# Fused attention and two MLPs: softmax transposes moved to the ends of slots, a pair's value products gathered in one slot, the norm's transposes in every other slot, the opening slots reordered

## The chip, the cores and the metric

One core of one Trainium2 chip runs the whole program. The metric is the device time of one execution in microseconds (us), the median of several runs. TensorE is written PE, VectorE DVE, ScalarE ACT, GpSimd POOL, and SyncE, which issues most of the DMAs, SP.

## The reference

The inputs are q, k and v of shape (4, 8, 576, 64), and the weights of two MLPs. All arrays are fp32.

```
scores = q @ k^T / sqrt(64)                        # per batch and head
scores = where(0 <= i - j < 128, scores - slope_h * |i - j|, -1e9)
a = exp(scores - max(scores)); a = a / (sum(a) + 1e-9)
x = (a @ v), heads side by side                    # (2304, 512)
h = x @ w_in                                       # (2304, 2048)
y = (h * clip(h + 3, 0, 6) / 6) @ w_out            # (2304, 512)
xn = y / sqrt(mean(y*y) + 1e-6) * rms_g
out = (silu(xn @ w_gate) * (xn @ w_val)) @ w_out2  # inner width 1536
```

A query sees only the 128 keys up to itself, so a tile of 128 queries needs two tiles of keys.

## The kernel before, in words

The 2304 tokens are 18 tiles of 128, in six **blocks** of three tiles. The order of all instructions is written out by hand, and each engine runs its own queue in that order; waits come from the data and from the tiles' buffers alone.

**Products.** The MLPs' matmuls run in fp32r, each fp32 operand split into a high and a low part, with three products for one. A **slot** of the first MLP is one 128-wide piece `m` of the inner width for one block: `product1` (12 matmuls of 384 columns into `ps_h`, one buffer), the activation into `g` (ACT Relu L599, DVE L600, ACT cast L605, DVE subtraction L611), and `product2` (nine matmuls of 512 columns into three `ps_o` tiles) of the slot before, which `finish1` issues. `PARTS` gives the order: block 0 up to piece 12, block 1, the rest of block 0, then blocks 2 to 5. Slots are counted by `t`; the first 15 (`AHEAD`) hold attention alone, the other 96 hold products too. The second MLP follows with no attention in it.

**Attention** runs in the slots ahead of the block that needs it. Two heads are a **pair**; a pair of a block has three **steps**, one for each tile of queries, u = 0, 1, 2. A step goes through S (scores on PE, `bias` on DVE, `exp` on ACT, the reciprocal `r` on POOL), D (`divide`, DVE), T (up to four transposes on PE into `ps_t`, and `weights`, the copy to `pt` on ACT) and V (`values`, up to eight matmuls into the pair's `ps_av`). After the last V, `finish` casts the pair's result on ACT and DVE. Q is the scaling (L247) or splitting (L253 to L260) of the pair's q and k. The table `plan` says in which slot, counted from the pair's first slot `t0`, each step does each part. Pairs of blocks 0 and 1 take three slots and overlap; those of blocks 2 to 5 (16 pairs) take four. Inside a slot of the first MLP, PE's order is `product1`, T, S, V, `product2`, then the norm's transposes.

**Norm.** When a block's first MLP is done, `Norm` evicts the three `ps_o` tiles, squares each (ACT L446), takes the factor on POOL, scales (DVE L454), transposes (four transposes into `ps_x`, issued by `back` at a slot's end) and copies (`store`, ACT L460, at the next slot's start; then a DMA to DRAM), one tile a slot. `ps_t` and `ps_x` are the same single PSUM buffer "T", so a transpose into it waits for the ACT copy of what stood there.

**Weights.** First-MLP weights come as 16 units of raw words, converted by ACT and DVE (`W1.step`, L116 to L132) through the slots of block 0. Second-MLP weights are converted through blocks 2 to 4 (`W2.finish`, the same lines, ACT's L130 writing a single buffer `wt`) and stored to DRAM by SP; when the last block of the first MLP starts, POOL fetches the first two converted tiles back (`W2.fetch`, L209) into space that attention has used.

**Opening.** Before the first slot, `busy(WARM)` issues five matmuls on a constant (each runs as two), and each of the 15 opening slots has one more, so that PE isn't idle. In an opening slot DVE's order is bias, the end of `finish`, the q scaling, divide.

Of the kernel before, what the change touches and what calls it, by code (L numbers as in the profile page):

```python
# [21 lines left out]
B, H, S, D = 4, 8, 576, 64  # L22
# [5 lines left out]
M1, M2 = F1 // P, F2 // P  # L28
# [7 lines left out]

CUT = 12

WARM = 5
PARTS = [(0, 0, CUT), (1, 0, M1), (0, CUT, M1)] + [(b, 0, M1) for b in range(2, len(BLOCKS))]  # L40

STARTS = {b * S // P for b in range(B) if b * S % P == 0}
# [4 lines left out]
PARTS_OF = ((0, 0), (0, 1), (1, 0))  # L47

AHEAD = 3 * H // 2 + 3

OPEN = {"reuse_waits": "tile"}


def f32(ap):
    return ap.bitcast(F32)
# [3 lines left out]
def fused_kernel(ctx: ExitStack, tc: tile.TileContext, qd, kd, v, w1, w2, rms_g, out):  # L59
# [10 lines left out]
    wpool = ctx.enter_context(tc.tile_pool(name="wpool", bufs=M1))  # L70
# [144 lines left out]
    W1, W2 = First(), Second()  # L215
# [143 lines left out]

    pairs = [Pair(b, j) for b in range(len(BLOCKS)) for j in range(H // 2)]
    slots = {kind: {} for kind in "QSDTV"}
    for k, pr in enumerate(pairs):
        b, j = divmod(k, H // 2)
        if b < 2:
            t0, plan = 3 * j if b == 0 else AHEAD - 3 + 3 * j, {"S": (0, 1, 2), "D": (1, 2, 3), "T": (2, 3, 4), "V": (3, 4, 5)}
        else:
            t0, plan = AHEAD + M1 * (b - 1) - 4 + 4 * j, {"S": (0, 0, 2), "D": (1, 1, 3), "T": (2, 3, 4), "V": (4, 4, 6)}
        slots["Q"].setdefault(t0 - 1, []).append(pr)  # L370
        for u in range(pr.n):
            step = Step(pr, u)
            for kind, at in plan.items():
                slots[kind].setdefault(t0 + at[u], []).append(step)

    def at(t):
        return [slots[kind].get(t, []) for kind in "QSDTV"]

    def prepare(pairs_, steps):

        for pr in pairs_:
            pr.split() if pr.parts else pr.scale()
        for x in steps:
            k = pairs.index(x.pair) + 2
            if x.last and k < len(pairs):
                pairs[k].load()
# [26 lines left out]
    def product2(outs, g, w, m, last, first=0):  # L413

        for i, o in enumerate(outs):
            for a, b in ((0, 0), (0, 1), (1, 0)):
                pe.matmul(  # L417
                    o,
                    lhsT=g[:, a, i * P : (i + 1) * P],
                    rhs=w[:, b],  # L420
                    start=(m == first and a == 0 and b == 0),
                    stop=(m == last and a == 1),
                )

    class Norm:
# [28 lines left out]
                vec.tensor_scalar(self.y[t], self.y[t], self.ri[t], None, ALU.mult)  # L454

        def store(self):
            k = self.t - 2
            if k in self.ps:
                yt = ypool.tile([P, KC, P], F32, tag="yt", name="yt", bufs=2)
                act.copy(yt, self.ps.pop(k))  # L460
                i = BLOCKS[self.b][0] + k
                d = dram.tile([P, KC, P], F32, tag=f"x2_{i}", name=f"x2_{i}")
                sp.dma_start(out=d, in_=yt)
                x2[i] = d
# [26 lines left out]
    def busy(n):  # L491
        for _ in range(n):
            pe.matmul(warm[:, : 2 * P], lhsT=rel[:, :P], rhs=rel, start=True, stop=True)  # L493

    busy(WARM)
    pairs[0].scale()
    for t in range(AHEAD):
        q, s_, d_, t_, v_ = at(t)
        scores(s_, t % 2)
        for x in t_:  # L500
            x.transpose()
        for x in v_:
            x.values()
        busy(1)
        for x in t_:
            x.weights()
        for x in s_:
            x.bias()
        for x in v_:
            if x.last:  # L510
                x.pair.finish()
        prepare(q, s_)
        for x in d_:
            x.divide()
        for x in s_:
            x.exp()
        if t == 2:
            W1.load(3)
        W1.step(0, *{4: (0,), 5: (1, 2), 7: (3,), 9: (4, 5)}.get(t, ()))
        W1.step(1, *{8: (0,), 11: (1, 2)}.get(t, ()))  # L520


    pend = None
    norms, partial = [], []

    def finish1():

        nonlocal outs
        b, m, m0, m1, g = pend
        if m == m0:  # L530
            outs = [ps_out.tile([P, DM], F32, tag="o", name="ps_o") for _ in range(BLOCKS[b][1])]
        product2(outs, g, W1.w_out(m), m, m1 - 1, m0)
        norms[:] = [x for x in norms if x.back()]
        if m == M1 - 1:
            norms.append(Norm(b, outs, partial if m0 else None))
        elif m == m1 - 1:
            for i, o in enumerate(outs):
                y = x0pool.tile([P, DM], F32, tag=f"part{i}", name="part")
                if i % 2:
                    act.activation(y, o, AF.Copy, scale=1.0 / 6.0)  # L540
                else:
                    vec.tensor_scalar(y, o, 1.0 / 6.0, None, ALU.mult)
                partial.append(y)

    def load_x2(b):
        i0, n = BLOCKS2[b]
        raw = p2x.tile([P, KC, 3 * P], F32, tag="x2raw", name="x2raw")
        for i in range(n):
            sp.dma_start(out=raw[:, :, i * P : (i + 1) * P], in_=x2[i0 + i])
        return raw  # L550
# [8 lines left out]
        )  # L559
        return t  # L560

    outs, slot = None, AHEAD
    for p, (b, m0, m1) in enumerate(PARTS):
        n = BLOCKS[b][1]
        last = p == len(PARTS) - 1
        nq = n * P
        if p == 2:
            conv.close()
            ypool = ys.enter_context(tc.tile_pool(name="ypool", bufs=3, **OPEN))
        if last:  # L570
            second.close()
            ys.close()
            att.close()
            ypool = p2.enter_context(tc.tile_pool(name="ypool2", bufs=3, **OPEN))
            wpool2 = p2.enter_context(tc.tile_pool(name="wpool2", bufs=2, **OPEN))
            p2x = p2.enter_context(tc.tile_pool(name="p2x", bufs=1, **OPEN))
            W2.fetch(2, wpool2)
        xs = xs_of[b]
        for m in range(m0, m1):
            t, slot = slot, slot + 1  # L580
            q, s_, d_, t_, v_ = at(t)
            if p == 3 and m == 2:
                first.close()
                wcpool = second.enter_context(tc.tile_pool(name="wcpool", bufs=1, side="right", **OPEN))
                W2.load()
                W2.load()
            for x in norms:
                x.store()
            ps = ps_h.tile([P, 4 * P], F32, tag="h", name="ps_h")
            product1(ps, W1.w_in(m), xs, n)  # L590
            for x in t_:
                x.transpose()
            if s_:
                scores(s_)
            for x in v_:
                x.values()
            g = gpool.tile([P, 2, 3 * P], F32R, tag="g", name="g")
            r = gpool.tile([P, 3 * P], F32, tag="t", name="t", bufs=1)
            act.activation(r[:, :nq], ps[:, :nq], AF.Relu, bias=three)  # L599
            vec.scalar_tensor_tensor(out=r[:, :nq], in0=r[:, :nq], scalar=6.0, in1=ps[:, :nq], op0=ALU.min, op1=ALU.mult)  # L600
            for x in t_:
                x.weights()
            for x in d_:
                x.divide()
            act.copy(g[:, 0, :nq], r[:, :nq])  # L605
            for x in s_:
                x.bias()
            for x in v_:
                if x.last:
                    x.pair.finish()  # L610
            vec.tensor_sub(g[:, 1, :nq], r[:, :nq], f32(g[:, 0, :nq]))  # L611
            for x in s_:
                x.exp()
            for x in norms:
                x.scale()
            prepare(q, s_)
            if p < 2:
                k = m + 1 if p == 0 else CUT + 1 + m
                W1.load(k + 3)
                if k < M1:  # L620
                    W1.step(k + 1, 0)
                    W1.step(k, 3, 4)
                    W1.step(k + 1, 1, 2)
                    W1.step(k, 5)
            if p == 3 and m == 3:
                W2.begin()
            if not last and (p == 3 and m > 3 or p > 3 and m % 4 != 0):
                W2.finish()
            if last:
                if m == M1 - 4:  # L630
                    raw = load_x2(0)
                if m == M1 - 1:
                    xs2 = [split_x2(0, raw, c) for c in range(KC)]
            if pend:
                finish1()
                if last and m:
                    W2.fetch(1, wpool)
            pend = b, m, m0, m1, g


# [13 lines left out]
    for b, (_, n) in enumerate(BLOCKS2):  # L654
        nq = n * P
        xs, xs2 = xs2, []
        for m in range(M2):
# [24 lines left out]
            pend = b, m, g  # L682
# [43 lines left out]
```

## Time and profile before

| | us |
|---|---|
| median of 3 runs | 1025.15 (1024.11 to 1025.45) |
| the profiled execution's own time | 1025.17 |
| its span, first to last instruction | 1023.4 |

The profile is of one execution. "Busy" is the time in which an engine has an instruction in flight; a timeline row gives the start, the time, the engine and its line, output and inputs, the count of merged instructions, and in brackets the idle time before it with what ended it. PE's matmuls overlap at their ends, so the length of a group is read from its start to the next group's start. "PEclk" is the granted share of TensorE's 2.4 GHz.

### The profile page before, as it was taken

What the parts mean: (1) busy time and instruction counts of PE and PEld (TensorE: products, weight loads), DVE (VectorE), ACT (ScalarE), POOL (GpSimd) and SP (SyncE); (2) the same over time, 40 slices, a digit from 0 to 9 for tenths busy, and PEclk for the clock granted to TensorE, in tenths of its full rate; (3) what the DMA queues carried; (4) which work ended last, traced back from release to release, by engine and by line L of the source; (5) the groups of instructions that cost most, each with busy time, mean ns of one, the idle gap of its engine ahead of it and who ended that gap; (6) DMA issues with size and microseconds to landing.
All of it is one profiled execution on the core that took longest, in us unless ns stands there. A gap on an engine that the chain in (4) does not pass through costs nothing.

```text
span 1023.4 us, 14712 instructions
## 1 busy us (share of the span) xinstructions
PE 1001.1 (98%) x5668; PEld 885.4 (87%) x5668; DVE 458.5 (45%) x1096; ACT 433.0 (42%) x952; POOL 115.5 (11%) x219
## 2 busy tenths in 40 slices
PE   8999899999999999999999999999999999999998
PEld 5577688888888788788899899999999999999997
DVE  5588764355787677766422312222222222222212
ACT  5699854356667665764432422112111122111111
POOL 4233111122212211220211100000000000000000
PEclk9899999999999999999999999999999999999999
DMA  6445401113675565543597300100100100200000
GB/s 216 136 183 195 191 29 32 55 39 125 210 234 179 186 210 175 189 160 124 200 334 247 124 21 1 62 1 1 62 1 1 62 1 1 62 2 1 31 1 31
DMA packets 49238, 105.28 MB, mean 103 GB/s; under 512 B 3856, under 2 KB 28432, under 8 KB 44816
## 3 DMA queue, kind: packets, MB, share of 16 engines
q1 hardware_dynamic: 46576, 85.47, 24.8%
q0 software_dynamic: 2592, 18.88, 5.5%
q8 instruction: 44, 0.72, 0.3%
q14 instruction: 26, 0.21, 0.1%
HBM read 76.02 MB, written 28.31 MB: 102 GB/s over the span
## 4 chain that ended last, share of the span: by engine, by line
PE 87%; DVE 6%; ACT 5%; issue 2%; DMA 1%; POOL 0%; ACTq 0%; POOLq 0%; DVEq 0%
PE ps_o L417 31%; PE ps_h L404 16%; PE ps_g L404 15%; PE ps_v L404 15%; PE ps_av L349 3%; PE ps_t L336 3%; PE ps_s L296 2%; PE ps_s L287 1%; DVE wx L128 1%; ACT w L130 1%; PE warm L493 1%; DVE t L600 1%; ACT wx L121 1%; DVE w L132 1%; ACT t L599 1%
## 5 line engine op out<-in xcount | busy, mean ns | idle before, releaser
L417 PE MATMUL ps_o<-w,g 128*128 128x512 f32 x1512 | 385.0, 398 | 5.6 <-DVE w L132 2.8
L417 PEld LDWEIGHTS ps_o<-w,g 128*128 128x128 f32 x1512 | 277.5, 188 | 67.6 <-DVE w L132 5.4
L404 PE MATMUL ps_h<-xs,w 128*128 128x384 f32 x1152 | 219.6, 338 | 1.8 <-DVE t L600 1.7
L404 PEld LDWEIGHTS ps_h<-xs,w 128*128 128x128 f32 x1152 | 203.5, 188 | 9.6 <-DVE t L600 2.6
L667 DVE TENSOR_TENSOR t<-t,ps_v 128x384 f32<-128x384 f32 x72 | 39.9, 554 | 306.0 <-PE ps_v L404 306.0
L404 PE MATMUL ps_g<-xs,w 128*128 128x384 f32 x864 | 163.8, 337 | 0.4 <-ACT xs L555 0.2
L404 PE MATMUL ps_v<-xs,w 128*128 128x384 f32 x864 | 161.5, 334 | 0.0
L404 PEld LDWEIGHTS ps_g<-xs,w 128*128 128x128 f32 x864 | 153.1, 188 | 7.4 <-ACT xs L555 0.7
L404 PEld LDWEIGHTS ps_v<-xs,w 128*128 128x128 f32 x864 | 151.0, 188 | 0.0
L600 DVE SCALAR_TENSOR_TENSOR t<-t,ps_h 128x384 f32<-128x384 f32 x96 | 53.2, 554 | 148.1 <-ACT t L599 148.1
L664 ACT ACTIVATE t<-ps_g 128x384 f32<-128x384 f32 x72 | 35.4, 492 | 192.5 <-PE ps_g L404 192.3
L669 ACT CAST g<-t 128x384 fp32r<-128x384 f32 x72 | 36.9, 513 | 162.3 <-DVE t L667 162.3
L599 ACT ACTIVATE t<-ps_h,three 128x384 f32<-128x384 f32 x96 | 55.2, 575 | 102.7 <-PE ps_h L404 102.5
L322 ACT ACTIVATE t<-t,m 128x256 f32<-128x256 f32 (+1 forms) x144 | 69.2, 483 | 11.9 <-DVE m L310 11.9
L324 POOL TENSOR_SCALAR r<-den 128x2 f32<-128x2 f32 x72 | 28.9, 402 | 341.3 <-ACT t L322 339.9
L130 ACT CAST w<-wx 128x512 fp32r<-128x512 f32 (+1 forms) x52 | 39.1, 751 | 57.8 <-DVE wx L128 42.5
L605 ACT CAST g<-t 128x384 fp32r<-128x384 f32 x96 | 49.3, 514 | 33.0 <-DVE t L600 26.9
L325 POOL TENSOR_TENSOR r<-r,minus 128x2 f32<-128x2 f32 x72 | 59.3, 823 | 6.0
L611 DVE TENSOR_TENSOR g<-t,g 128x384 fp32r<-128x384 f32 x96 | 53.2, 554 | 13.1 <-ACT g L605 12.0
L670 DVE TENSOR_TENSOR g<-t,g 128x384 fp32r<-128x384 f32 x72 | 40.2, 558 | 41.7 <-ACT g L669 41.7
L132 DVE TENSOR_TENSOR w<-wx,w 128x512 fp32r<-128x512 f32 (+1 forms) x52 | 44.1, 848 | 13.4 <-ACT w L130 13.4
L310 DVE CUSTOM_DVE_ANT_0 t<-ps_s,rel 128x256 f32<-128x256 f32 (+2 forms) x128 | 44.8, 395 | 10.7 <-PE ps_s L296 9.0
(63 smaller groups left out, 711.5 us busy)
## 6 DMA issues: line engine op xcount, KB each, us to landing
wraw<-w SPq DMA_DIRECT2D x36, 512.0 KB, 4.6
w<-w SPq DMA_DIRECT2D x36, 512.0 KB, 3.2
w<-w POOLq DMA_DIRECT2D x18, 1024.0 KB, 5.3
wraw<-w SPq DMA_DIRECT2D x16, 1024.0 KB, 8.7
kraw<-kd SPq DMA_DIRECT2D x20, 256.0 KB, 2.7
vraw<-v SPq DMA_DIRECT2D x20, 256.0 KB, 4.1
qraw<-qd SPq DMA_DIRECT2D x24, 192.0 KB, 2.8
x<-yt SPq DMA_DIRECT2D x18, 256.0 KB, 2.2
```

Of the source, the lines that this page charges most:

```text
L130: act.copy(t[:, 0], x)
L132: vec.tensor_sub(t[:, 1], x, f32(t[:, 0]))
L310: vec.tensor_tensor_reduce(out=self.t[:, a, c0:], in0=s[:, c0:], in1=(rel_split if self.i in SPLITS else rel)[:, c0:], scale=2.0 ** (-8.0 ...
L322: act.activation(p, p, AF.Exp, bias=self.m[:, a : a + 1], scale=-1.0, accum_out=self.den[:, a : a + 1])
L325: pool.tensor_tensor(self.r, self.r, minus, ALU.pow)
L404: pe.matmul(ps[:, : n * P], lhsT=w[:, a, c * P : (c + 1) * P], rhs=xs[c][:, b, : n * P], start=(k == 0), stop=(k == 3 * KC - 1),)
L417: pe.matmul(o, lhsT=g[:, a, i * P : (i + 1) * P], rhs=w[:, b], start=(m == first and a == 0 and b == 0), stop=(m == last and a == 1),)
L599: act.activation(r[:, :nq], ps[:, :nq], AF.Relu, bias=three)
L600: vec.scalar_tensor_tensor(out=r[:, :nq], in0=r[:, :nq], scalar=6.0, in1=ps[:, :nq], op0=ALU.min, op1=ALU.mult)
L605: act.copy(g[:, 0, :nq], r[:, :nq])
L611: vec.tensor_sub(g[:, 1, :nq], r[:, :nq], f32(g[:, 0, :nq]))
L670: vec.tensor_sub(g[:, 1, :nq], r[:, :nq], f32(g[:, 0, :nq]))
```

## The change

The plan of blocks 2 to 5 becomes: T of u = 1 in slot `t0 + 3` as before, behind `product1` and with no scores in that slot; T of u = 0 and u = 2 under a new kind L, issued behind `product2` (and the norm's transposes) at the very end of slots `t0 + 1` and `t0 + 3`, their `weights` copies on ACT at the next slot's start (`late`); V of all three steps in slot `t0 + 4`, which is the next pair's `t0`. `finish` of a pair so falls in the same slot. The norm's `scale` and `back` run only in slots an even number past the 15th (`go`) from block 2 on, in every slot before that and in the last block; `store` copies whatever was transposed. `finish1` moves ahead of `W1.step` and `W2.finish` in program order. In the opening and block 0, Q moves one slot earlier for the pairs of blocks 0 and 1; q scaling and divide go ahead of `finish`; `WARM` is 3.

```diff
-WARM = 5
+WARM = 3
...
-            t0, plan = AHEAD + M1 * (b - 1) - 4 + 4 * j, {"S": (0, 0, 2), "D": (1, 1, 3), "T": (2, 3, 4), "V": (4, 4, 6)}
-        slots["Q"].setdefault(t0 - 1, []).append(pr)
+            t0, plan = AHEAD + M1 * (b - 1) - 4 + 4 * j, {"S": (0, 0, 2), "D": (1, 1, 3), "T": (None, 3, None), "L": (1, None, 3), "V": (4, 4, 4)}
+        slots["Q"].setdefault(t0 - (2 if b < 2 else 1), []).append(pr)
...
         def store(self):
-            k = self.t - 2
-            if k in self.ps:
+            for k in list(self.ps):
...
+        prepare(q, s_)
+        for x in d_:
+            x.divide()
         for x in v_:
             if x.last:
                 x.pair.finish()
-        prepare(q, s_)
-        for x in d_:
-            x.divide()
...
-        norms[:] = [x for x in norms if x.back()]
+        if go:
+            norms[:] = [x for x in norms if x.back()]
...
+            go = p < 3 or last or (t - AHEAD) % 2 == 0
...
+            for x in late:
+                x.weights()
+            late = l_
             ps = ps_h.tile([P, 4 * P], F32, tag="h", name="ps_h")
             product1(ps, W1.w_in(m), xs, n)
...
-            for x in norms:
-                x.scale()
+            if go:
+                for x in norms:
+                    x.scale()
             prepare(q, s_)
+            if pend:
+                finish1(go)
+                if last and m:
+                    W2.fetch(1, wpool)
+            for x in l_:
+                x.transpose()
...
-            if pend:
-                finish1()
-                if last and m:
-                    W2.fetch(1, wpool)
```

## Rows read from the trace of the kernel before

**Rows 1.** The page, busy time of the engines over the span.
```profile
PE 1001.1 (98%) x5668; PEld 885.4 (87%) x5668; DVE 458.5 (45%) x1096; ACT 433.0 (42%) x952; POOL 115.5 (11%) x219
```
**Rows 2.** Waits of PE: total us, times, longest us.
```profile
PE ps_t L336 <- ACT yt L460: 4.9, 4, 1.5
PE ps_s L296 <- DVE qraw L247: 2.9, 4, 0.9
...
PE ps_o L417 <- ACT part L540: 2.6, 1, 2.6
...
PE ps_h L404 <- DVE t L600: 1.7, 1, 1.7
```
**Rows 3.** Timeline of PE: slots of one pair, and a slot with values alone.
```profile
362.36 2.27 PE L404 MATMUL ps_h<-xs,w 128*128 128x384 f32 x12
364.46 0.60 PE L336 MATMUL ps_t<-ident,t 128*128 128x128 f32 x4
364.99 0.98 PE L287 MATMUL ps_s<-ks,qs 64*128 64x256 f32 x12
365.90 1.09 PE L349 MATMUL ps_av<-pt,vraw 128*64 128x128 f32 x16
366.92 2.34 PE L417 MATMUL ps_o<-w,g 128*128 128x512 f32 x9
369.10 2.27 PE L404 MATMUL ps_h<-xs,w 128*128 128x384 f32 x12
...
373.29 2.27 PE L404 MATMUL ps_h<-xs,w 128*128 128x384 f32 x12
...
379.20 2.27 PE L404 MATMUL ps_h<-xs,w 128*128 128x384 f32 x12
...
383.83 2.27 PE L404 MATMUL ps_h<-xs,w 128*128 128x384 f32 x12
...
484.17 2.27 PE L404 MATMUL ps_h<-xs,w 128*128 128x384 f32 x12
486.37 0.66 PE L349 MATMUL ps_av<-pt,vraw 128*64 128x128 f32 x8
486.95 2.33 PE L417 MATMUL ps_o<-w,g 128*128 128x512 f32 x9
```
**Rows 4.** Timeline of DVE: divides in the slot that starts at 369.10.
```profile
372.49 1.14 DVE L330 TENSOR_SCALAR t<-t,r 128x256 f32<-128x256 f32 x4
```
**Rows 5.** Timeline of PE and ACT around the norm of block 2.
```profile
336.28 0.66 PE L336 MATMUL ps_t<-ident,t 128*128 128x128 f32 x4 [1.53 <-ACT yt L460]
...
335.04 0.62 ACT L446 ACTIVATE junk<-y 128x512 f32<-128x512 f32 x1
...
335.65 0.57 ACT L460 COPY yt<-ps_x 128x512 f32<-128x512 f32 x1
```
**Rows 6.** Timeline of PE in the opening slots.
```profile
2.17 4.63 PE L493 MATMUL warm<-rel 128*128 128x256 f32 x10 [2.17 <-POOL rel L93]
...
19.39 0.49 PE L296 MATMUL ps_s<-kraw,qraw 64*128 64x128 f32 x4 [0.87 <-DVE qraw L247]
```
**Rows 7.** Stretches: us, busy by engine, PEclk, DMA share, GB/s.
```profile
33.00:35.20 2.20, 1.40 (x12) 0.71 (x10) 1.36 (x7) 2.00 (x9) 0.92 (x2) 1.00 0.69 210
35.20:42.30 7.10, 7.04 (x30) 3.94 (x30) 3.82 (x16) 3.39 (x9) 2.39 (x4) 0.52 0.12 37
```
**Rows 8.** Timeline of PE and DVE in slots 28 to 30, behind block 0's first part.
```profile
131.17 2.27 PE L404 MATMUL ps_h<-xs,w 128*128 128x384 f32 x12
...
130.26 1.14 DVE L330 TENSOR_SCALAR t<-t,r 128x256 f32<-128x256 f32 x4
...
141.31 0.61 DVE L330 TENSOR_SCALAR t<-t,r 128x256 f32<-128x256 f32 x2
```
**Rows 9.** Timeline of ACT and POOL at the last block's start.
```profile
497.46 0.62 ACT L130 CAST w<-wx 128x512 fp32r<-128x512 f32 x1 [4.25 <-DMA w<-w]
...
487.36 1.32 POOL L209 DMA_DIRECT2D w<-w  x2 [16.53 <-PE ps_av L349]
```

More of the change, by code (lines that the diff above doesn't have):

```diff
@@ L49 @@
 AHEAD = 3 * H // 2 + 3
+KINDS = "QSDTLV"
 OPEN = {"reuse_waits": "tile"}
@@ L362, in fused_kernel @@
     pairs = [Pair(b, j) for b in range(len(BLOCKS)) for j in range(H // 2)]
-    slots = {kind: {} for kind in "QSDTV"}
+    slots = {kind: {} for kind in KINDS}
     for k, pr in enumerate(pairs):
@@ L373, in fused_kernel @@
             for kind, at in plan.items():
-                slots[kind].setdefault(t0 + at[u], []).append(step)
+                if at[u] is not None:
+                    slots[kind].setdefault(t0 + at[u], []).append(step)
     def at(t):
-        return [slots[kind].get(t, []) for kind in "QSDTV"]
+        return [slots[kind].get(t, []) for kind in KINDS]
     def prepare(pairs_, steps):
@@ L497, in fused_kernel @@
     for t in range(AHEAD):
-        q, s_, d_, t_, v_ = at(t)
+        q, s_, d_, t_, _, v_ = at(t)
         scores(s_, t % 2)
@@ L524, in fused_kernel, with finish1 @@
     norms, partial = [], []
-    def finish1():
+    def finish1(go=True):
         nonlocal outs
@@ L560, in split_x2 @@
         return t
-    outs, slot = None, AHEAD
+    outs, slot, late = None, AHEAD, []
     for p, (b, m0, m1) in enumerate(PARTS):
@@ L580, in fused_kernel @@
             t, slot = slot, slot + 1
-            q, s_, d_, t_, v_ = at(t)
+            q, s_, d_, t_, l_, v_ = at(t)
+            go = p < 3 or last or (t - AHEAD) % 2 == 0
             if p == 3 and m == 2:
```

## The prediction

> **What bounds the kernel now.** I read the page first: PE is busy for 98% of the span [rows 1], so only what PE does, or waits for, can move the end. The second view is the waits of PE. They are few and have four main causes: a softmax transpose that waits for the norm's copy out of the shared PSUM buffer (4.9 us), scores that wait for the scaled q (2.9 us), a product that waits for the eviction of block 0's partial result (2.6 us) and one that waits for an activation (1.7 us) [rows 2]. The third is PE's timeline, which gives each group's price as the distance from its start to the next group's start [rows 3]. The reader is to see how regular this is: a slot without attention takes 4.19 us (369.10 to 373.29), whatever other engines do. The fourth is the granted clock by stretches: it is 1.00, 2.4 GHz, but for one stretch of 7.1 us in the opening at 0.52, mostly the 1.2 GHz level, right behind a stretch in which PE was busy for 1.40 of 2.20 us [rows 7]. So the change is worth what it takes out of PE's row: waits, the price of groups, and the slow stretch.
>
> **Values in one slot.** Sixteen matmuls of V take 1.02 us (365.90 to 366.92), eight take 0.58 (486.37 to 486.95) [rows 3]: 0.44 for each further eight, 0.14 once. A pair had 16 in one slot and 8 in another, 1.60 us; 24 together are 1.46 by that line. 16 pairs x 0.14 = 2.3 us. If instead each step costs 0.58 wherever it stands, 24 cost 1.74, and 2.3 us are lost; if the fixed part is twice what I read, 4.5 are gained. I take 2.3, on the line through the two rows.
>
> **Transposes moved.** T ahead of scores costs 0.53 us (364.46 to 364.99). T with nothing else in its slot makes that slot 4.63 instead of 4.19 (379.20 to 383.83): 0.44. Scores or values that stand directly behind product 1 begin 2.20 after its start (484.17 to 486.37), transposes 2.10 (362.36 to 364.46): 0.10 more [rows 3]. So taking T from ahead of S saves 0.53 and costs 0.44 + 0.10: nothing. The trace has no scores that follow product 1 in these slots, so I keep 0.1 either way for 2 T in 16 pairs, +-3 us.
> What a T at a slot's end can lose is a wait: all behind it in PE's queue, the next slot's product 1 first, stands still. T of u = 0 now ends slot t0 + 1, whose divides come late: in the slot that starts at 369.10 they start at 372.49 and take 1.14 us for four [rows 4]. The two of u = 0 are done at about 373.06; T's place is behind product 2, at 373.29 [rows 3]. The cover is 0.23 us, so I cost it at nothing. T of u = 2 has only its own two divides ahead of it and a T of u = 1 in its slot: more cover. The copies of these T run on ACT at the next slot's start, ahead of its Relu, while PE is in product 1 for 2.1 us; V, their first reader, stands behind the scores.
>
> **The norm.** T of u = 1 waited up to 1.53 us for the copy of the norm's tile, since ACT had a square (335.04) and a weight piece ahead of the copy (335.65, 0.57 us) [rows 5]. Every other slot leaves only the second tile of a block with a T in the middle of the next slot. There ACT now has the square ahead of the weight piece, filling what was idle time, and `finish` is gone from that slot on DVE and ACT; I estimate that 0.15 remains, in three blocks (none to 1.5 each). One new wait comes: in slot 46 `go` still holds in each slot, a norm's transpose and a T follow each other directly, and the second must wait for the copy between them, 0.57 plus about 0.2 for the hand-over. Sum: 4.9 - 0.45 - 0.75 = 3.7 us (0 to 4.9).
>
> **The opening.** Four matmuls of the warm-up go: ten took 4.63 us [rows 6], so 1.85 us if PE stays at that slow pace, half of it (0.9) if the clock rises at the same moment as before. The first softmax chain on DVE, ACT and POOL then becomes the limit for a moment; I take 1.2 (0.5 to 1.9). q is scaled a slot earlier, and scaling and divide no longer stand behind `finish`, so the waits as at 19.39 go [rows 2, 6]: 2.9 at most. ACT is close to full in these slots, and the divide that follows the scaling is the next in line, so I take 2.2 (0 to 2.9). The slow stretch came right behind the last of these waits. With PE denser it should not come: 7.1 us x 0.48 = 3.4 at most [rows 7]; I take 3.0 (0, or -3.4 for a second such stretch). Together 6.4. The later Q moves are 0.4 us of DVE work each, moved from one slot to its neighbour: nothing.
>
> **Evictions ahead of the weight pieces.** In slot 27 the partial result is evicted before the conversions on ACT and DVE, so the 2.6 us wait [rows 2] goes. But the same conversions now delay the next activation, and with it the divides of slot 28, which start at 130.26 [rows 8]. T of u = 0 at that slot's end needs two of them, 130.85, and with its own 0.36 product 1 of slot 29 starts at 131.2, against 131.17 before: nothing gained. Slot 30 repeats it: its product 1's buffer and its divides hang on the same activation, and T of u = 2 must wait until the divides of 141.31 have run for 0.61 us [rows 8], where product 1 could start at their beginning before: about 1.0 lost. I take -1.0 (-1.5 to +2.6).
>
> **The fetch.** The last weight conversion waited 4.25 us for an earlier store (until 497.46), since two fetches, issued at 487.36 when the last V had run, filled the DMA engines [rows 9]; PE paid the 1.7 us on L600 [rows 2]. The last V is now two slots earlier, and so is the fetch, in slots with a single store behind it: 1.7 gained (0 to 1.7).
> The Trainium skill (Trainium Kernel Development and Optimization, Key Constraints) says that DMAs from SP's and POOL's queues share the same engines and interleave. By it the fetch will slow whatever is in flight two slots earlier as well; if that again ends at the conversion, this term is 0 and the sum 1.7 smaller.
>
> **Sum.** 2.3 + 3.7 + 6.4 - 1.0 + 1.7 = 13.1 us off the profiled 1025.17, which is the median of the runs within 0.02: 1012.
>
> **The rivals.**
> 1. *The clock falls all the same*, or rises later for the shorter warm-up. For it: transposes and short matmuls fill the opening. Against: the waits in it go. Price 3.0: 1015. Chance 0.17. The Trainium skill (TensorE: Matmul & The Clock Gate, Part 4) says that PE's transposes don't count as activity as other matmuls do; no row here separates them.
> 2. *The opening's lead is lost in block 0*, where ACT and DVE convert weights and PE waits for them: if these set the pace from the opening on, 6.4 goes: about 1018.5. Against: they start from what slot 15 gives them, so a lead should carry. Chance 0.11.
> 3. *The norm's copy stays late* behind ACT's weight pieces: three waits of about 1.5 remain, and slot 46: 1015.7. Chance 0.10.
> 4. *T at the end of slot t0 + 1 waits for its divides* in every pair. The cover is 0.23 us; what would eat it is ACT: the copies it now runs ahead of the Relu, or `finish` between bias and exp. One copy of 0.57 in the way makes 16 x 0.34 = 5.4 us: 1017.5; from a lateness of 0.23 + 13.1 / 16 = 1.05 on, the kernel is no faster than before, and at 1.5 us it takes 1032. Chance 0.10, of which 0.04 past that point.
> 5. *Bunching saves nothing*: V costs 0.58 for each step: 1012 + 4.6 = 1016.7. Chance 0.05.
> The forecast has 0.47.
>
> **Numbers.** Forecast 1012, by itself 1008 to 1015 (norm, opening and fetch at their ends). Rivals 1, 2, 3 and 5 and the mild part of 4 lie below 1019, two of them together at about 1021; the low end takes all opening terms and no loss in block 0: 1006. The range 1006 to 1021 leaves out the bad part of 4 and three mishaps together. 0.2% of the time is 2 us, about what a measurement of this kernel can tell from no change. Faster by more than that: everything but rival 4's end and several mishaps, 0.92; within 0.2%: 0.04; slower: 0.04.
>
> **What would show it.** In the profile after: no granted clock under 1 before the end; scores in the opening without waits for the q scaling; slots of 4.63 us for t0 + 1; one group of 24 V of about 1.46 us; a single wait of about 0.75 for the norm's copy near slot 46 and none above 0.3 elsewhere; no wait of 4 us for a store on ACT near the last block's start. The prediction is wrong if `ps_t` waits for DVE's `t` in each pair, if PE's waits for L132 in block 0 grow by what the opening gained, or if the slow stretch is still there.

## The result and the profile after

The changed kernel takes 1012.4 us, the median of four runs (1011.39 to 1014.86); the kernel before took 1025.12 beside it. The ratio is 0.9881, with a 95% interval of 0.9862 to 0.99. The forecast was 1012, the range 1006 to 1021: the time was met. Its parts were not all met, and two of them missed in opposite directions.

The profiled execution of the kernel after is the longest of its four, 1014.86 us with a span of 1013.1. The page gives PE's busy time, beside 1001.1 before [rows 1]:

```profile
PE 996.4 (98%) x5664; PEld 880.4 (87%) x5664; DVE 458.1 (45%) x1096; ACT 434.0 (43%) x952; POOL 115.5 (11%) x219
```

PE is busy for 4.7 us less; the rest of the 10.3 us between the spans is idle time of PE that is gone. The waits of PE after (total us, times, longest):

```profile
PE ps_t L338 <- DVE t L332: 4.5, 4, 2.3
PE ps_o L421 <- DVE w L134: 2.3, 5, 0.8
...
PE ps_t L338 <- ACT yt L463: 1.4, 3, 0.7
PE ps_av L351 <- ACT pt L343: 1.1, 3, 0.4
PE ps_h L408 <- DVE t L608: 0.4, 1, 0.4
```

Beside [rows 2], the waits for the scaled q, for the partial result and the one of 1.7 us on DVE's activation line are gone, and the norm's copy costs 1.4 instead of 4.9. Values that wait for the copy of a transposed tile (1.1) are new. Two more lines of the view before are needed beside the first two rows after:

```profile
PE ps_o L417 <- DVE w L132: 2.8, 6, 0.8
...
PE ps_t L336 <- DVE t L330: 0.2, 1, 0.2
```

Transposes that wait for divides have grown from 0.2 to 4.5. Product 2's wait for converted weights, in block 0, was larger than two of the four causes that the prediction lists, and the prediction leaves it out; the change hardly touches it (2.3).

PE's timeline in block 2, a pair and the slot behind it, answers to [rows 3]:

```profile
358.56 0.98 PE L289 MATMUL ps_s<-ks,qs 64*128 64x256 f32 x12
359.46 1.53 PE L351 MATMUL ps_av<-pt,vraw 128*64 128x128 f32 x24
360.92 2.34 PE L421 MATMUL ps_o<-w,g 128*128 128x512 f32 x9
...
363.46 2.36 PE L408 MATMUL ps_h<-xs,w 128*128 128x384 f32 x12
365.66 2.25 PE L421 MATMUL ps_o<-w,g 128*128 128x512 f32 x9
367.74 0.60 PE L338 MATMUL ps_t<-ident,t 128*128 128x128 f32 x4
368.10 2.35 PE L408 MATMUL ps_h<-xs,w 128*128 128x384 f32 x12
...
381.23 1.09 PE L351 MATMUL ps_av<-pt,vraw 128*64 128x128 f32 x16
382.66 0.66 PE L351 MATMUL ps_av<-pt,vraw 128*64 128x128 f32 x8 [0.34 <-ACT pt L343]
```

Twenty-four values take 1.46 us (359.46 to 360.92), the slot with a T at its end takes 4.64 (363.46 to 368.10), and that T, at 367.74, waits for nothing: all three as forecast. The last two rows are not: in this pair the 24 values are broken in two, and the last eight wait. ACT's timeline shows why:

```profile
380.92 0.62 ACT L132 CAST w<-wx 128x512 fp32r<-128x512 f32 x1 [2.73 <-DMA w<-w]
381.44 0.70 ACT L123 ACTIVATE wx<-wraw 128x512 f32<-128x512 f32 x1
382.05 0.56 ACT L343 COPY pt<-ps_t 128x512 f32<-128x512 f32 x1
```

A weight piece on ACT (L132 writes the single buffer that a store must have left) waits 2.73 us for that store. The copy of T's tile, put off to the next slot's start, stands two instructions behind it.

In the opening, PE waits twice for divides instead of four times for q, and at slot 46 for the norm's copy:

```profile
25.78 0.63 PE L338 MATMUL ps_t<-ident,t 128*128 128x128 f32 x4 [0.43 <-DVE t L332]
...
31.75 0.43 PE L338 MATMUL ps_t<-ident,t 128*128 128x128 f32 x2 [1.20 <-DVE t L332]
...
224.73 0.66 PE L338 MATMUL ps_t<-ident,t 128*128 128x128 f32 x4 [0.73 <-ACT yt L463]
```

The stretches of [rows 7] after (us, busy by engine, PEclk, DMA share, GB/s) have no slow clock:

```profile
33.00:35.20 2.20, 2.20 (x15) 1.20 (x14) 2.16 (x7) 2.20 (x6) 0.75 (x3) 1.00 0.47 146
35.20:42.30 7.10, 7.04 (x49) 4.74 (x49) 4.41 (x18) 5.10 (x17) 3.38 (x8) 1.00 0.29 84
```

Slot 28, behind block 0's first part, holds the longest wait of the kernel after; PE first, then ACT and DVE. It is to be read beside [rows 8]:

```profile
125.56 0.63 PE L338 MATMUL ps_t<-ident,t 128*128 128x128 f32 x4 [2.27 <-DVE t L332]
...
137.09 0.63 PE L338 MATMUL ps_t<-ident,t 128*128 128x128 f32 x4 [0.62 <-DVE t L332]
...
122.97 1.12 ACT L123 ACTIVATE wx<-wraw 128x1024 f32<-128x1024 f32 x1
124.00 0.56 ACT L607 ACTIVATE t<-ps_h,three 128x384 f32<-128x384 f32 x1
...
125.06 1.14 DVE L332 TENSOR_SCALAR t<-t,r 128x256 f32<-128x256 f32 x4
```

`ps_h` has been full since about 121, but ACT's Relu comes only at 124.00, behind the conversions of weight pieces. DVE's divides stand behind that activation, T behind the divides, and product 1 of slot 29 behind T.

Last, the fetch, beside [rows 9]: POOL issues it 16.8 us earlier (half of that is the lead that this kernel has by then, see the ledger below), and the last conversion waits only for DVE, for no store.

```profile
470.58 1.32 POOL L211 DMA_DIRECT2D w<-w  x2 [7.47 <-PE ps_av L351]
...
486.10 0.62 ACT L132 CAST w<-wx 128x512 fp32r<-128x512 f32 x1 [1.30 <-DVE wx L130]
```

**A ledger by slots.** Product 1 (`ps_h`) starts once in each slot, so its start can be compared between profiled executions. The table gives how much earlier than in the kernel before it starts, in us. Five of the runs told below stand beside the kernel after.

| slot | after | five warm-ups | opening alone | old table | spread, copies at once | before with spread |
|---|---|---|---|---|---|---|
| 15 (opening done) | 4.97 | 5.24 | 6.22 | 4.77 | 6.82 | 3.95 |
| 28 | 5.17 | 5.44 | 6.46 | 4.99 | 7.00 | 3.91 |
| 31 | 3.98 | 4.22 | 5.11 | 4.99 | 9.76 | 6.99 |
| 43 | 4.55 | 4.79 | 5.18 | 4.96 | 10.33 | 7.07 |
| 47 (slot 46 done) | 3.72 | 3.96 | 5.18 | 4.96 | 9.50 | 7.07 |
| 95 (blocks 2 to 4 done) | 8.40 | 11.13 | 5.19 | 10.26 | 16.83 | 7.09 |
| 97 (fetch done) | 10.32 | 12.95 | 5.17 | 8.35 | 18.63 | 7.13 |

### The profile page after: what moved, and what is told of

Its sections match the earlier page's. It is cut to its first block, busy times and chain, and to the rows that moved or that the text cites. A ratio compares the mean times of both kernels' runs of the same rounds, so it can differ in the third digit from the quotient of the medians.

```text
span 1013.1 us, 14695 instructions
## 1 busy us (share of the span) xinstructions
PE 996.4 (98%) x5664; PEld 880.4 (87%) x5664; DVE 458.1 (45%) x1096; ACT 434.0 (43%) x952; POOL 115.5 (11%) x219
## 4 chain that ended last, share of the span: by engine, by line
PE 82%; DVE 7%; ACT 6%; DMA 3%; issue 3%; POOL 0%; ACTq 0%; POOLq 0%; DVEq 0%
PE ps_o L421 29%; PE ps_g L408 15%; PE ps_v L408 15%; PE ps_h L408 14%; DMA w<-w 3%; PE ps_av L351 2%; PE ps_t L338 2%; DVE wx L130 2%; ACT wx L123 2%; PE ps_s L298 2%; ACT w L132 1%; ACT t L607 1%; PE warm L496 1%; DVE t L332 1%; DVE t L608 1%
## 5 line engine op out<-in xcount | busy, mean ns | idle before, releaser
L408 PEld LDWEIGHTS ps_h<-xs,w 128*128 128x128 f32 x1152 | 200.9, 188 | 5.4 <-DVE t L608 0.8
L132 ACT CAST w<-wx 128x512 fp32r<-128x512 f32 (+1 forms) x52 | 39.1, 752 | 52.0 <-DVE wx L130 27.5
L327 POOL TENSOR_TENSOR r<-r,minus 128x2 f32<-128x2 f32 x72 | 57.2, 794 | 6.0
L338 PE MATMUL ps_t<-ident,t 128*128 128x128 f32 x272 | 42.6, 277 | 6.0 <-DVE t L332 4.5
```

What stands on the lines that cost most here:

```text
L132: act.copy(t[:, 0], x)
L327: pool.tensor_tensor(self.r, self.r, minus, ALU.pow)
L338: pe.transpose(self.ps[:, a, c], self.t[:, a, c * P : (c + 1) * P], ident)
L408: pe.matmul(ps[:, : n * P], lhsT=w[:, a, c * P : (c + 1) * P], rhs=xs[c][:, b, : n * P], start=(k == 0), stop=(k == 3 * KC - 1),)
```

## The experiments

All runs, each with the kernel before timed on the same chip:

| run | median us (range, runs) | before | ratio (95%) |
|---|---|---|---|
| opening alone | 1020.64 (1019.1 to 1022.39, 10) | 1024.88 | 0.997 (0.9959 to 0.998) |
| old table | 1016.26 (1013.12 to 1017.1, 4) | 1024.88 | 0.9919 (0.9895 to 0.9944) |
| norm in each slot | 1023.37 (1022.11 to 1025.3, 10) | 1024.88 | 0.9994 (0.9983 to 1.0005) |
| pieces first | 1012.21 (1011.4 to 1013.29, 4) | 1024.88 | 0.989 (0.9874 to 0.9906) |
| first pair old | 1011.69 (1010.82 to 1013.14, 4) | 1023.12 | 0.9892 (0.9877 to 0.9906) |
| tail spread | 1007.94 (1007.33 to 1009.45, 4) | 1023.12 | 0.9856 (0.9841 to 0.9871) |
| copies at once | 1011.54 (1010.14 to 1012.4, 4) | 1023.12 | 0.9884 (0.9868 to 0.9901) |
| old table but last | 1011.98 (1011.02 to 1012.79, 4) | 1023.12 | 0.9893 (0.9878 to 0.9907) |
| spread, copies at once | 1006.51 (1006.09 to 1008.09, 4) | 1023.44 | 0.9834 (0.9819 to 0.9849) |
| the same, two pairs | 1005.9 (1005.42 to 1008.27, 4) | 1023.44 | 0.983 (0.981 to 0.985) |
| before with spread | 1018.53 (1018.05 to 1018.97, 4) | 1023.44 | 0.9948 (0.9934 to 0.9963) |
| five warm-ups | 1012.43 (1012.23 to 1012.92, 4) | 1023.44 | 0.989 (0.9875 to 0.9904) |

**1. The opening alone**, on the kernel before:

```diff
-WARM = 5
+WARM = 3
...
-        slots["Q"].setdefault(t0 - 1, []).append(pr)
+        slots["Q"].setdefault(t0 - (2 if b < 2 else 1), []).append(pr)
...
+            if x.last:
+                x.pair.finish()   # in the opening, behind divide
```

> The kernel before with the opening's edits alone (three warm-up matmuls, q scaled a slot earlier, scaling and divide ahead of finish). If the opening's lead carries through block 0: 5 to 6.5 us faster, 1018.5 to 1020, with product 1 of slot 15 at about 40 us instead of 45.4 and that of slot 31 ahead by the same amount. If the weight conversions of block 0 set the pace (the rival that loses the lead there): 1024 to 1025, with the waits for L132 grown by 5 us. If the clock falls all the same: about 1022.

Measured: 0.3% faster (0.2 to 0.41%), 2 to 4.2 us, less than the 5 to 6.5 expected. The profile has 6.22 us at slot 15 and carries them to slot 28 (6.46), so block 0 doesn't eat the lead; rival 2 is out. It then loses 1.35 by slot 31. PE waits there for the partial result as long as in the kernel before (2.61 against 2.64 us), but here the product behind the wait runs at half the clock:

```profile
122.53 3.91 PE L417 MATMUL ps_o<-w,g 128*128 128x512 f32 x9 [2.61 <-ACT part L540]
```

Nine such matmuls take 2.33 us at the full clock (129.54 in this trace).

**2. The old table** in the kernel after:

```diff
-"T": (None, 3, None), "L": (1, None, 3), "V": (4, 4, 4)}
+"T": (2, 3, 4), "V": (4, 4, 6)}
```

> The changed kernel with the old table for softmax transposes and values (T at 2, 3, 4 and V at 4, 4, 6), all else kept. Theory: a pair costs 0.14 us more (2.3 in all), the fetch at the last block's start collides with the store again (1.7), and the wait of 2.3 us for divides in slot 28 with its sequel goes (-1.2): about 1015.2. If bunching the values saves nothing: about 1013. If moving the transposes was itself the gain, more than 0.3 us a pair: over 1018.

Measured: 1016.26, 3.9 us above the kernel after, though the two intervals overlap. The ledger tells where: up to slot 95 the old table is even 1.86 us ahead of the kernel after's profile (and 0.87 behind that of run 12); then it loses 1.91 where the other gains 1.92. Its trace at the fetch (PE, ACT, POOL):

```profile
489.46 3.91 PE L408 MATMUL ps_h<-xs,w 128*128 128x384 f32 x12 [2.05 <-DVE t L608]
...
487.60 0.62 ACT L132 CAST w<-wx 128x512 fp32r<-128x512 f32 x1 [4.65 <-DMA w<-w]
...
477.10 1.32 POOL L211 DMA_DIRECT2D w<-w  x2 [16.53 <-PE ps_av L351]
```

The wait of 4.25 us for the store [rows 9] is back, PE pays 2.05, and the product behind it takes 3.91 us instead of 2.27: the clock has fallen. It does not fall in each execution: two of the four runs, 1013.12 and 1015.68 us, have a mean granted clock of 1.000.

**3. The norm in each slot**, in the kernel after:

```diff
-            go = p < 3 or last or (t - AHEAD) % 2 == 0
+            go = True
```

> The changed kernel with the norm in every slot again. Theory: in each of blocks 0, 2 and 3 a norm transpose and a softmax transpose meet at a slot's end and the second waits 0.7 us for the copy between them, and a T in mid-slot waits up to 1 us: 3 to 5 us slower, 1015.5 to 1017.5. If the waits of before came from the order of ACT's weight pieces alone, which stays changed here: within 1 us of the changed kernel.

Measured: 1023.37, 11 us above the kernel after, where 3 to 5 were expected, and no longer faster than before. With the new table, a norm's transposes and a T stand next to each other at a slot's end, with one PSUM buffer for both. PE's and ACT's timelines at one of the two worst places, and the windows (us, busy by engine, PEclk, DMA share, GB/s):

```profile
333.36 0.60 PE L475 MATMUL ps_x<-ident,y 128*128 128x128 f32 x4
337.00 0.77 PE L338 MATMUL ps_t<-ident,t 128*128 128x128 f32 x4 [3.03 <-ACT yt L463]
337.41 3.89 PE L408 MATMUL ps_h<-xs,w 128*128 128x384 f32 x12
...
335.28 0.62 ACT L132 CAST w<-wx 128x512 fp32r<-128x512 f32 x1 [1.78 <-DVE wx L130]
335.81 0.66 ACT L123 ACTIVATE wx<-wraw 128x512 f32<-128x512 f32 x1
336.38 0.56 ACT L463 COPY yt<-ps_x 128x512 f32<-128x512 f32 x1
...
330.00:337.40 7.40, 3.83 (x23) 2.91 (x22) 5.77 (x12) 4.90 (x10) 1.02 (x3) 1.00 0.75 268
337.40:341.00 3.60, 3.60 (x15) 3.58 (x13) 0.00 (x0) 0.59 (x1) 0.00 (x0) 0.53 0.58 220
```

The copy that frees the buffer stands behind a weight piece that itself waits for DVE. Six waits of this kind cost 8.7 us, and three times in this execution the clock falls behind a wait for 3.4 us, twice behind one of these six and once behind slot 28's wait for divides. Half the clock for 3.4 us is 1.7 us of work at most.

**4. The weight pieces first**: `finish1` and the L transposes are moved in program order behind `W1.step` and `W2.finish`, as `finish1` stood before.

> The changed kernel with product 2, the norm and the transposes at slots' ends issued behind the weight pieces again, as before. PE's own order does not change. Theory: the square of the norm falls behind ACT's piece, the T after a norm's second tile waits 0.6 us longer in three blocks (+1.8), and the partial result is evicted late again (a wait of 2.6 us), but the wait of 2.3 us for the divides in slot 28 shrinks by as much: 1013.5 to 1014.5. If the eviction's place matters by itself: 1015 or more.

Measured: 1012.21, the same as the kernel after and less than the 1013.5 to 1014.5 expected. The old wait for the partial result is there again (2.6 us) and the waits for divides shrink from 4.5 to 2.0, all of them in the opening; in the times one is as dear as the other. The longer waits expected behind a norm's second tile did not come: the norm's copy makes PE wait once, 0.73 us at slot 46. So what freed those waits is the norm's place in every other slot and not the order of ACT's pieces.

**5. The first pair of block 2 on the old table**, the rest as after:

```diff
+        if k == 2 * (H // 2):
+            plan = {"S": (0, 0, 2), "D": (1, 1, 3), "T": (2, 3, 4), "V": (4, 4, 6)}
```

> The changed kernel with the old table for the first pair of block 2 alone, whose transposes met the weight conversions in slots 28 to 30. Theory: the waits of 2.3 and 0.6 us for divides go, but product 1 of slots 29 and 30 now waits for the activation instead; at slot 31 the kernel is about 1 us earlier than the changed one: 1011.4. If the transposes' place was not what lost time there: 1012.4 or more.

Measured: 1011.69, not to be told from the kernel after. The wait at slot 28 only changes its owner: T's waits for divides fall to 2.4 in all, none of them behind the opening, and `ps_h` waits 1.9 for the activation instead.

**6. The tail spread.** Before and after alike, what is left of weight units 13 to 15 is converted in slots 27 to 29. Here it is cut into ten pieces, one in each of slots 29 to 38; block 1 needs the first of them in slot 40:

```diff
+TAIL = [(13, 3, 4), (13, 5), (14, 0), (14, 1, 2), (14, 3, 4), (14, 5), (15, 0), (15, 1, 2), (15, 3, 4), (15, 5)]
...
-                if k < M1:
+                if p == 1 and 2 <= m < 2 + len(TAIL):
+                    W1.step(*TAIL[m - 2])
+                if p == 0:
                     W1.step(k + 1, 0)
```

> The changed kernel with the last three units of first-MLP weights converted in ten pieces over slots 29 to 38 instead of three slots, 27 to 29. Theory: ACT and DVE are the bound in slots 27 to 30, so all waits there go: 3.5 to 4.5 us at slot 31, 1008 to 1009, and no fall of the clock near 125 us. If PE itself is the bound there or the pieces only move the wait: within 1 us of the changed kernel.

Measured: 1007.94, 3.6 to 4 us below the three others timed on the same chip with it, with ranges that don't overlap. The waits for divides in slots 28 and 30 and for the activation are gone.

**7. The copies at once**: ACT issues L's copies directly behind the transposes, ahead of the weight pieces, and not at the next slot's start.

```diff
             for x in l_:
                 x.transpose()
+            if p > 2:
+                for x in l_:
+                    x.weights()
```

> The changed kernel with the copies of transposes at slots' ends issued on ACT at once, ahead of the weight pieces of the same slot, from block 2 on (before that as in the changed kernel). Theory: a pair of the split-score blocks loses 0.1 to 0.6 us because V waits for the third copy behind a weight piece that waits for its store; 1 to 2 us faster, 1010.5 to 1011.5, and values in one group of 1.46 us in all pairs. If ACT loses as much by waiting for the transposes at the slot's end (Relu later, divides later): within 0.5 us.

Measured: 1011.54, the ratio that of the kernel after. No value waits for `pt` in its trace. But runs 5 and 6 have no such wait either, with the copies late: it depends on when the store lands, from one execution to the next.

**8. The old table for all pairs but the last**, the last as after:

```diff
+        if 2 * (H // 2) <= k < len(pairs) - 1:
+            plan = {"S": (0, 0, 2), "D": (1, 1, 3), "T": (2, 3, 4), "V": (4, 4, 6)}
```

> The changed kernel with the old table for all pairs but the last, which keeps its values in one slot. Theory: the table itself lost about 2 us by the last block's start, and its one gain of size is the early fetch, which needs the last pair alone: 1 to 2 us faster than the changed kernel, 1010.5 to 1011.5. If bunching gains 0.14 us a pair as I forecast: 1014 to 1015.

Measured: 1011.98, the same as the kernel after, and neither of the two times expected. From slot 28 to 95 its profile gains 5.68 us, and that of run 12, with the new table throughout, 5.69: what the values gain, T gives back in slots 28 to 30 and 46. So the new table as a whole is worth what its last pair does to the fetch.

**9. Spread and copies at once together**, from runs 6 and 7.

> The kernel after with two edits together: the last three weight units converted in ten pieces in slots 29 to 38, and L's copies issued by ScalarE at once behind the transposes. Theory (the two losses are separate: the wait of slots 28 to 30 for late VectorE operations, and the wait of the values for the copy that stands behind ScalarE's store): alone they gave 4.5 and 0.9 us, together about 5.0 to 5.4, 1007.0 to 1007.5 us. Rival (the pieces' spread had already moved the store's wait away, since its profile has no wait of ps_av for pt): no more than the spread alone, 1007.9 us.

Measured: 1006.51, 1.4 below the spread alone, though the intervals overlap, so the rival isn't out. Slot 28 after the spread, PE and ACT:

```profile
119.19 2.25 PE L423 MATMUL ps_o<-w,g 128*128 128x512 f32 x9
121.28 0.60 PE L340 MATMUL ps_t<-ident,t 128*128 128x128 f32 x4
121.63 2.36 PE L410 MATMUL ps_h<-xs,w 128*128 128x384 f32 x12
...
118.35 0.57 ACT L546 ACTIVATE part<-ps_o 128x512 f32<-128x512 f32 x1
119.39 0.58 ACT L609 ACTIVATE t<-ps_h,three 128x384 f32<-128x384 f32 x1 [0.46 <-PE ps_h L410]
```

ACT waits for PE here and not the other way round, and T follows product 2 with no wait.

**10. The same, with two pairs on other tables**: the first pair of block 2 on the old one, and the pair of slot 43 with its later T in slots 46 and 47 and its values in slots 47 and 49.

```diff
+        if k == 3 * (H // 2):
+            plan = {"S": (0, 0, 2), "D": (1, 1, 3), "T": (None, 3, 4), "L": (1, None, None), "V": (4, 4, 6)}
```

> The run above, with the pair of slots 27 to 33 on the old table, and the pair of slot 43 with two transposes in later slots and its values in slots 47 and 49. Theory: what is left of TensorE's waits between slots 28 and 48 is the 0.73 us ahead of slot 46's last transposes; that wait goes, and the table as such is worth nothing, so 0.5 to 0.9 us faster than the run above. Rival (what is taken from one slot comes back in the next, as with the old table for all pairs): within 0.3 us of the run above.

Measured: 1005.9, the fastest kernel here, 1.7% below the one before. The wait of 0.73 us at slot 46 is gone, but of the 0.62 us that it is ahead of run 9 at slot 47, 0.17 are left at slot 95; the two runs are not to be told apart.

**11. The kernel before with the tail spread alone.**

> The kernel before with the spread of the last three weight units alone. Theory (the gain of the spread is that of ScalarE and VectorE in slots 28 to 31 and has nothing to do with the new table): about 3 to 4.5 us faster than before, 1020.5 to 1022 us. Rival (the spread pays only because the new table put transposes behind those operations): within 1 us of before.

Measured: 0.52% faster (0.37 to 0.66%), 1018.53, more than the 3 to 4.5 us expected. Its profile gains 3.08 us from slot 28 to 31, so the spread needs nothing of the change. This run also holds the opening of the kernel before unchanged, and there its profile shows 1.00 where [rows 7] have 0.52:

```profile
33.00:35.20 2.20, 1.33 (x8) 0.60 (x8) 1.78 (x5) 2.20 (x6) 1.08 (x3) 1.00 0.70 232
35.20:42.30 7.10, 7.04 (x51) 4.40 (x50) 4.49 (x20) 5.29 (x17) 2.84 (x7) 1.00 0.16 43
```

**12. Five warm-up groups** in the kernel after (`WARM = 5`).

> The kernel after with five warm-up groups in place of three. Theory (two groups of 0.6 us are TensorE time on the path of the opening): 0.9 to 1.9 us slower, 1013.3 to 1014.3 us. Rival (the opening waits for its loads and for the clock, and a warm-up group that fills such a wait costs nothing): within 0.5 us of 1012.4.

Measured: 1012.43, not to be told from the kernel after (the ratios' intervals overlap for the most part). Its slot 15 starts at 40.16, 0.28 us earlier than in the kernel after. But the clock rises at 6.6 us here and at 11.2 there. The three profiles with three groups that rise at 6.6 to 6.8 us (runs 1, 6 and 10) start slot 15 at 39.17 to 39.83. So at the same clock the two groups cost 0.3 to 1.0 us, less than these medians can show.

## Why the prediction was right

The time was right because the mechanism of each term was there and the errors in size cancelled. That they cancelled was luck, and so, in part, was the time that the gain is taken from: the four executions of the kernel before beside the result took 1024.11 to 1025.45 us, the seven beside runs 5 to 8 have a median of 1023.12. The profiled run with five warm-ups, 1012.23 us, is nearest to the median of the kernel after; its program differs by two warm-up groups alone, and its ledger adds up to 12.95 of the 12.94 us between it and the profiled 1025.17; the terms are read from it.

- **Values in one slot**, forecast 2.3. From slot 31 to 43, three pairs gain 0.57. From slot 47 to 95 the new table gains 7.17 and the old one 5.30, so 12 pairs gain 1.87, or 0.16 each against 0.14, moved transposes included. Right, and the 1.46 us of the 24 values in one group show it by themselves; rival 5 is out. In the kernel after's own profile this gain is lost again: from slot 47 to 95 it gains 4.68, 2.5 less, and seven of its slots there are longer by 2.55 together than in run 12. The wait for `pt` is in three of them, the wait for the norm's copy in two. The loss is about what this execution is above the median, 2.46 us; that the other three executions lack it isn't shown. The working counted ACT's copies as covered by product 1; a copy put off behind a weight piece that waits for a store isn't.
- **Moving T**, forecast 0. In the regular pairs that holds: T at the end of slot t0 + 1 doesn't wait for its divides outside slots 28 and 30. Rival 4, a wait in each pair, is out.
- **The norm**, forecast 3.7, was too small. With the old table, where slot 46 costs nothing, the gain from slot 47 to 95 is 5.30; slot 46 takes 0.83 from it with the new one (4.79 to 3.96). That leaves 4.5. The rest of a wait that I put at 0.15 a block is 0.34 at 265.93, and 0.3 and 0.1 in the next two blocks of this profile; run 12 has none. Rival 3 is out: the copy's waits are 1.4 in all. The gain with the old table is larger than the 4.9 that the waits' view had, and the trace of the kernel before shows one reason. This is product 1 ahead of the wait of 1.53 in [rows 5]:

```profile
332.39 2.36 PE L404 MATMUL ps_h<-xs,w 128*128 128x384 f32 x12
```

  T follows 3.89 us later (at 336.28), where 2.10 is the distance without a wait: 1.79 us lost for 1.53 of idle time, since a group that doesn't wait starts before the one ahead has ended. Four such waits cost about 1 us more than their idle time. The rest of the account stays open.
- **The opening**, forecast 6.4, was too large in the times. At slot 15 the twelve profiles with the new opening are 4.68 to 6.96 us ahead of the profile before, but alone the edits are worth 2 to 4.2 in the times (run 1's profile loses 1.35 of its lead again to the fall of the clock behind slot 28's wait). Its three parts: the warm-up, 1.2, is 0.3 to 1.0 in profiles and not seen in the times (run 12). The q waits went, but two waits for divides, 0.43 and 1.20, came; that loss was named as the next in line and priced at 0.7. The slow clock, 3.0, is the step that failed. Runs 9 and 11 rise to the full clock at the same time (5.5 us) and have no fall, and their slots 15 start at 38.59 and 41.46: the new opening is worth 2.87 when the clock is the same, against 3.4 for the first two parts. The remainder, 3.95, lies between two executions of the old opening, those of run 11 and of the profile before: the second rises to the full clock 2.4 us later and falls from it once. So the fall does not belong to the old opening. Whether the new one makes it rarer is open: none of its twelve profiles has it, and one of two with the old opening.
- **Evictions**, forecast -1.0: -1.2 in both ledgers from slot 28 to 31. Right, by the chain that was written down: conversions, activation, divides, T. In the kernel after's ledger slot 28 is worth nothing, as forecast, since PE's 2.27 for divides stand in place of the 2.64 for the partial result, and slot 30 loses 1.05. Run 6 shows that neither was needed: this corner was worth 4 us more, in the kernel before too (run 11), and I didn't look for that.
- **The fetch**, forecast 1.7: 1.82 to 1.92 from slot 95 to 97. The Trainium skill (Trainium Kernel Development and Optimization, Key Constraints) says that DMAs from SP's and POOL's queues share the same engines and interleave, which the prediction held against this term; in the kernel after's trace the DMA engines' share is 0.97 in the 4.4 us behind the fetch at 470.58, and the last conversion still has no wait for a store.

Rival 1, a clock that falls all the same, came in part, only not in the opening and not at its price: in run 12, whose program there is that of the kernel after, the clock falls behind the wait at slot 28, and in the kernel after's profile it doesn't. The windows of the kernel after, and then those of run 12:

```profile
120.00:126.10 6.10, 3.83 (x21) 3.11 (x21) 5.34 (x10) 5.27 (x9) 2.48 (x3) 1.00 0.00 0
126.10:129.50 3.40, 3.40 (x20) 2.74 (x20) 2.92 (x5) 2.27 (x3) 0.00 (x0) 1.00 0.02 5
```

```profile
120.00:126.10 6.10, 3.82 (x22) 3.10 (x21) 5.35 (x10) 5.26 (x8) 2.21 (x3) 1.00 0.00 0
126.10:129.50 3.40, 3.40 (x13) 2.96 (x12) 2.90 (x4) 2.27 (x3) 0.00 (x0) 0.50 0.02 5
```

PE is busy for 3.83 and 3.82 of the same 6.10 us, and then it runs at 2.4 GHz in one execution and at 1.2 GHz in the other. The slow stretch cost almost nothing: from slot 28 to 31 the ledger loses 1.19 without it and 1.22 with it. What the slow clock takes in slot 29 comes back in slot 30, where the kernel after waits 0.41 for the activation and 0.62 for divides and run 12 for neither. Left open is what decides between the two; whether the kernel after at its median has this fall can only be inferred from its other runs' mean granted clocks, 0.998, 0.998 and 0.999.

## What to carry to other kernels

Where PE sets the time, list for each of its instructions the queue of the engine that feeds it, weight pieces and stores included: moving the consumer later helps only until the feeder's own backlog ends, and here spreading that backlog gave 4 us that neither reordering tried here (runs 4 and 5) did. A buffer shared by two users needs the second user's copy ahead of long work on the copying engine, or a slot between them; run 3 lost 11 us, the falls of the clock behind such waits included. And a slow clock seen in one profile is one execution's: look at the mean clock of all runs before counting it as the program's, and at whether PE would have waited in its place.

## What was not expected of the hardware

- The clock's fall behind a wait of 2 to 3 us of PE is not fixed by the program, as the two pairs of windows above show. The programs of runs 5 and 8 are the same up to there, opening included. Product 1 of slot 29 in run 5 and then in run 8, behind the same wait:

```profile
124.06 3.02 PE L410 MATMUL ps_h<-xs,w 128*128 128x384 f32 x12 [1.95 <-DVE t L610]
```

```profile
125.35 2.35 PE L410 MATMUL ps_h<-xs,w 128*128 128x384 f32 x12 [1.95 <-DVE t L610]
```

  The clock falls during the first and not at the second. The runs of the kernel before agree: timed beside the first four runs, its 19 executions fall in two groups, eight from 1022.25 to 1023.49 us with a mean granted clock of 0.998, and eleven from 1024.84 to 1025.54 with 0.996 or 0.997. The four executions of run 11, without the long wait for the partial result, all have 1.000; of the 33 of the kernel before beside the experiments none has more than 0.998.
- The first rise to the full clock varies too, with the same first instructions. In the kernel after a group of four scores (L298, 64x256) still takes 1.23 us at 9.21; in run 4, whose PE queue is the same up to there, it takes 0.70 at 6.10. In the 11 profiles with three warm-up groups the rise comes from 5.1 to 6.8 us in seven and from 11.2 to 11.7 in four, in the three with five groups from 5.5 to 7.9. The four late ones start slot 15 at 40.44 to 40.73 us, the others at 38.45 to 39.83.
